# Where the second layer's weights are prepared: three units of w2_in in the last first-layer batch, the later ones one step later, five pieces of w2_out at the end of the h phase

## The chip, the cores and the metric

The kernel runs on one core of a Trainium2 chip. The metric is device time in microseconds, from the first to the last instruction of that core with what the launch adds around it. TensorE (PE) multiplies, VectorE (DVE), ScalarE (ACT) and GpSimd (POOL) do the elementwise work, and all transfers are issued from SyncE's queue (SP).

## The reference, cut to what matters

```python
x = attention(q, k, v, g_q, g_k)            # 4 batches, 12 heads, 448 tokens, 64 wide -> (1792, 768)
g = x @ w_gate;  val = x @ w_val             # 768 -> 1536
x = (g / (1 + exp(-g)) * val) @ w_out        # 1536 -> 768
h = x @ w2_in                                # 768 -> 2048
out = (h * cos(h)) @ w2_out                  # 2048 -> 768
```

The weights arrive as 64-bit floats and the results are wanted in float32, so most products are made of three fp16 matmuls on high and low halves (high x high, high x low, low x high).

## The kernel before, in words

The program has an attention part and three matmul phases. For each of the four batches the **first layer** runs 36 "pieces" of 18 matmuls: 24 of gate and val, 12 of out1 (w_out). The attention of the next batch is interleaved with it, so the last batch (the fourth) has no attention beside it; there DVE and ACT split the y results of the earlier batches instead. Then comes the **h phase** (w2_in): eight units c = 0 to 7, each two pieces of weights (k0 = 0 and 3), each used for all four batches b = 0 to 3. A step (c, b) is 36 matmuls of 448 columns into a pair of PSUM banks; four banks serve, so step n needs the banks of step n-2. I count steps from 0 to 31, step = 4c + b. At last the **out2 phase** (w2_out) multiplies the G2 tiles by 16 pieces of w2_out (two to a matmul piece).

A 64-bit weight piece goes through five stations: a load into a `raw` tile (L818), three DVE instructions that make float32 of it (L838 to L840), squares with a row sum on ACT (L858), a PE matmul that adds the rows of the unit's pieces (L865) followed by four short DVE instructions that make a power of two of the sum (L845 to L850), and a split into two fp16 halves, one instruction on ACT (L870) and one on DVE (L871). A `raw` tile is free again after the squares, because those write into it. Pieces of first use go through all this ("fresh"); a piece whose split was stored to DRAM is loaded as two halves (L892) into a `wp` tile.

`pre_step` prepares pieces ahead of their phase, one station of each of up to four pieces per call. Before, it is called 21 times (PRE: three times late in the third batch, every second piece of the fourth), and prepares all 16 pieces of w2_out as float32 in DRAM (`o32`); h pieces are not among them (NPH = 0). The h pieces are loaded at b = 0 of unit c (w_loads, L1270s), converted at b = 1, summed at b = 2 and split at b = 3, always four or five pieces ahead. The eviction of an h step (`fin_h`) is an ACT copy to integer (L1131), two DVE instructions (L1137, L1138), ACT Abs and Sin (L1139, L1140), a DVE product that reads PSUM for the last time (L1141), and the split of G2 on ACT and POOL (L1145, L1146). Its two scale rows come from a table (L1098, L1099).

The order of instructions on each engine is not the order of the code: a scheduler lays out the whole program and may put an instruction well ahead of the place where it was written. Each engine then works through its row in that order, and waits where an operand is late. SP does the same with transfers.

Of the kernel before, what the change touches and what calls it, by code (L numbers as in the profile page):

```python
# [11 lines left out]
F16 = mybir.dt.float16  # L12
# [10 lines left out]
LA = 5  # L23
CA = 4
# [8 lines left out]
CRW = 2  # L33
CSH = 10
VMQ = 2
PRE = {2: (30, 2), 3: (0, 2)}
NPH = 0
LO = 3
WSTEP = {4: [("load", 2)], 12: [("conv", 0)], 16: [("conv", 1), ("load", 3)], 19: [("scale", 1)], 20: [("split", 0), ("conv", 2), ("load", 4)],
         26: [("split", 1), ("conv", 3), ("load", 5)]}  # L40
# [99 lines left out]
def kernel(ctx: ExitStack, tc, q, k, v, g_q, g_k, w_gate, w_val, w_out, w2_in, w2_out, out):  # L140
# [23 lines left out]
    parts = {"raw": [raw_p, raw_p, raw_m], "wp": [wp_p, wp_p, wp_m]}  # L164
    turn = {"raw": 0, "wp": 0}

    def rot(nm):
        turn[nm] += 1
        return parts[nm][turn[nm] % 3]
    nm_p = ctx.enter_context(tc.tile_pool(name="nm", bufs=8))  # L170
# [616 lines left out]
    for c in range(H * D // CO):  # L787
        for b in range(0, B, 2):
            for k0 in range(0, FF2, 2):
                pieces.append(dict(kind="out2", b=b, c=c, k0=k0, n=2, first=k0 == 0, last=k0 == FF2 - 2))  # L790
    pre_load = [("out2", kt, 0) for kt in range(FF2)] + [("h", c, k0) for c in range(FF2 // 2 - NPH, FF2 // 2) for k0 in (0, 3)]
    scr = {}
    for pc in pieces:
        key = pc["key"] = (pc["kind"], pc["c"], pc["k0"])
# [10 lines left out]
    nrm_t = {}  # L805
    stores = []

    def wp_tile(dt):
        if dt == F16:
            return rot("wp").tile([P, 2, 768], F16, tag="wp", name="wp")  # L810
        return rot("wp").tile([P, 768], F32R, tag="wp", name="wp")

    sq_dst = [None]
# [60 lines left out]
    def w_load(j):  # L874
        if j >= len(pieces):
            return
        pc = pieces[j]
        if pc["kind"] == "out2" and pc["fresh"]:
            t = rot("raw").tile([P, 6 * 256], I32, tag="raw", name="raw")
            nc.sync.dma_start(t.bitcast(F32), o32[pc["k0"] // 2])  # L880
            for kk in range(2):
                w32_t[j, pc["k0"] + kk] = t[:, kk * 768:(kk + 1) * 768].bitcast(F32)
        elif pc["fresh"]:
            raw_t[j] = load64(WGT[pc["kind"]], pc["k0"], pc["c"], pc["n"], 256)
        elif pc["kind"] == "out1":
            wh, wl = wp_tile(F32R), wp_tile(F32R)
            nc.sync.dma_start(wh.bitcast(F32), scr[pc["key"]][:, 0])
            nc.sync.dma_start(wl.bitcast(F32), scr[pc["key"]][:, 1])
            wp_t[j] = (wh, wl)
        else:  # L890
            wp = wp_tile(F16)
            nc.sync.dma_start(wp, scr[pc["key"]])  # L892
            wp_t[j] = (wp[:, 0], wp[:, 1])
            wp_full[j] = wp
# [64 lines left out]
    pre_scale = []  # L959
    pre_split = []  # L960

    def pre_step():
        done = False
        if pre_split and (pre_split[0][0] == "out2" or len(pre_split) > 1):
            kind, c, k0, w32 = pre_split.pop(0)
            if kind == "h":
                for kind, c, k0, w32 in ((kind, c, k0, w32), pre_split.pop(0)):
                    stores.append((scr[kind, c, k0], split16(UNIT0[kind] + c, w32)))
            done = True
        if pre_scale and (pre_scale[0][0] == "out2" or len(pre_scale) > 1):  # L970
            kind, c, k0, w32 = pre_scale.pop(0)
            unit_scale(UNIT0[kind] + c)
            if kind == "h":
                pre_split.append((kind, c, k0, w32))
                pre_split.append(pre_scale.pop(0))
            done = True
        if pre_conv:
            kind, c, k0, rw = pre_conv.pop(0)
            w32 = conv64(rw)
            squares(UNIT0[kind] + c, w32)  # L980
            if kind == "out2":
                stores.append((o32[c // 2][:, c % 2 * 768:(c % 2 + 1) * 768], w32))
            pre_scale.append((kind, c, k0, w32))
            done = True
        if pre_load:
            kind, c, k0 = pre_load.pop(0)
            rw = load64(w2_out, c, 0, 1, 768) if kind == "out2" else load64(w2_in, k0, c, 3, 256)
            pre_conv.append((kind, c, k0, rw))
            done = True
        return done  # L990
# [212 lines left out]
    for b in range(B):  # L1203
# [14 lines left out]
        for qn in range(per):  # L1218
# [1 line left out]
            kind, c = pc["kind"], pc["c"]  # L1220
            w_store()
            w_loads(j + LA)
            if b in PRE and qn >= PRE[b][0] and (qn - PRE[b][0]) % PRE[b][1] == 0:
                pre_step()
            for i in sched.get(qn, ()):
                if b + 1 < B:
                    step(i, b + 1)
# [19 lines left out]
            wp_t.pop(j)  # L1247
            j += 1

    while pre_step():  # L1250
        w_store()
    w_store()
    g_ctx.close()
# [7 lines left out]
        y_get(B - 1, kt)  # L1261
    for kt in range(KX):
        y_split(B - 1, kt)
    w_scale(j + CA - 1)
    scaled = False
    for c in range(NH):
        j0 = j
        j += 2
        for b in range(B):
            ps = [bank(ps_m, "mm") for _ in range(2)]  # L1270
            for jj in range(j0, j):
                w_store()
                if b == 0:
                    w_loads(jj + LA)
                if b == 1:
                    w_conv(jj + CA)
                if b == 2:
                    w_scale(jj + CA)
                    if jj + CA >= N2 - 1 and not scaled:
                        out2_scales()  # L1280
                        scaled = True
                if b == 3:
                    w_split(jj + 2)
                mm_piece(jj, ps, lambda kt: Y[b, kt])
                if late:
                    late.pop(0)[1]()

            def fin(b=b, c=c, ps=ps):
                fins["h"](b, c, ps)
            if not (b == B - 1 and c == NH - 1):  # L1290
                late.append((0, fin))
            else:
                fin()
# [53 lines left out]
```

## Time and profile before

| | us |
|---|---|
| median of 3 runs (1375.33 to 1380.41) | 1379.12 |
| the profiled execution | 1378.04 |
| its span, first to last instruction | 1375.8 |
| PE busy in the span | 1198.8 (87%) |
| DVE busy | 850.9 (62%) |
| ACT busy | 658.7 (48%) |
| POOL busy | 404.5 (29%) |
| mean granted TensorE clock | 0.953 |

The profiled execution is 1.1 us below the median. The attention and first-layer part ends at 899.4 us, the h phase at about 1159, out2 at the end. A page row "idle ... <-ACT raw L858" says that the engine stood still until that instruction had ended. A "PEclk" of 1.00 is 2.4 GHz, 0.50 is 1.2 GHz.

### The profile page before, as it was taken

The numbers are of one execution on the slowest core, as the hardware profiler recorded it, in microseconds if no ns is written. First come the engines' busy times: TensorE is split into PE (matmuls) and PEld (weight loads), VectorE is DVE, ScalarE is ACT, GpSimd is POOL, SyncE is SP. The second block draws the span as 40 slices with busy tenths as digits, with TensorE's granted clock in tenths as the row PEclk, the third lists the DMA queues.
The fourth block names the chain that finished last, engine by engine and source line by source line (L and its number), as shares of the span: only waits on it lengthen the run. The fifth ranks groups of instructions, "written<-read, shape, count | busy, mean of one in ns | idle before, by whom it ended". The sixth has DMA issues, their size and how long they took to land. (4 is left out here: it accounts for less than half of the span.)

```text
span 1375.8 us, 18244 instructions
## 1 busy us (share of the span) xinstructions
PE 1198.8 (87%) x6454; PEld 676.4 (49%) x6454; DVE 850.9 (62%) x1556; ACT 658.7 (48%) x1282; POOL 404.5 (29%) x315
## 2 busy tenths in 40 slices
PE   0688677787896989999999998967999999999998
PEld 0233233334762435854458545943544555666665
DVE  6878968998947777437751676287888765200000
ACT  1567567775442645346552344265767776100000
POOL 7621345555832535214330011002233322000000
PEclk9999898788997899999999999988999999999999
DMA  7535568897999979989988988823210021633121
GB/s 233 143 81 139 183 158 245 224 247 220 287 331 286 218 172 259 302 206 203 208 190 256 322 313 274 303 74 100 73 54 24 11 62 68 217 122 98 58 87 41
DMA packets 262107, 243.93 MB, mean 177 GB/s; under 512 B 178048, under 2 KB 208256, under 8 KB 262016
## 3 DMA queue, kind: packets, MB, share of 16 engines
q1 hardware_dynamic: 262016, 242.77, 61.7%
q8 instruction: 50, 0.82, 0.2%
q14 instruction: 41, 0.34, 0.1%
HBM read 160.30 MB, written 42.51 MB: 147 GB/s over the span
## 5 line engine op out<-in xcount | busy, mean ns | idle before, releaser
L1001 PE MATMUL mm<-xy,wp 128*128 128x448 f16 x960 | 348.2, 364 | 34.2 <-DVE tmp L1141 10.0
L1002 PE MATMUL mm<-xy,wp 128*128 128x448 f16 x960 | 349.1, 364 | 0.0
L1003 PE MATMUL mm<-xy,wp 128*128 128x448 f16 x960 | 343.0, 362 | 6.0 <-DVE wp L871 5.9
L1014 PEld LDWEIGHTS <-g 128*128 128x128 f16 x1344 | 131.5, 98 | 87.3
L1001 PEld LDWEIGHTS <-wp 128*128 128x128 f16 x960 | 98.3, 102 | 121.3 <-issue 25.1
L1002 PEld LDWEIGHTS <-wp 128*128 128x128 f16 x960 | 96.3, 100 | 106.4 <-issue 30.5
L1003 PEld LDWEIGHTS <-wp 128*128 128x128 f16 x960 | 95.1, 100 | 102.5 <-issue 10.8
L1146 POOL TENSOR_TENSOR g<-tmp,g 128x448 f16<-128x448 f32 x64 | 71.5, 1136 | 230.7 <-ACT g L1145 150.8
L493 POOL TENSOR_TENSOR p<-pr,p 128x448 f16<-128x448 f32 x72 | 93.5, 1303 | 139.5 <-ACT p L484 105.3
L460 ACT ACTIVATE pr<-s,sm,esc 128x448 f32<-128x448 f32 x126 | 90.2, 718 | 67.2 <-DVE sm L454 58.5
L1001 PE MATMUL mm<-g,wp 128*128 128x448 f32 x288 | 108.8, 378 | 0.0
L1048 POOL TENSOR_TENSOR g<-tmp,g 128x448 fp32r<-128x448 f32 x48 | 63.9, 1343 | 150.5 <-ACT g L1047 150.4
L1002 PE MATMUL mm<-g,wp 128*128 128x448 f32 x288 | 106.5, 370 | 0.0
L1003 PE MATMUL mm<-g,wp 128*128 128x448 f32 x288 | 105.9, 369 | 0.0
L1014 PE MATMUL s<-wp,g 128*128 128x384 f16 x576 | 100.3, 326 | 0.0
L1014 PE MATMUL mm<-wp,g 128*128 128x384 f16 x576 | 99.2, 326 | 0.0
L450 DVE TENSOR_REDUCE sm<-s 128x1 f32<-128x448 f32 x126 | 75.4, 615 | 26.0 <-PE s L441 25.9
L484 ACT ACTIVATE p<-pr 128x448 f16<-128x448 f32 x126 | 69.8, 571 | 23.9 <-DMA PT<-p 22.8
L318 POOL TENSOR_TENSOR ri<-ss,half 128x14 f32<-128x14 f32 x24 | 63.7, 2660 | 57.2 <-DVE ss L316 48.4
L1157 ACT ACTIVATE tmp<-mm,osc 128x384 f32<-128x384 f32 x8 | 4.7, 581 | 148.6 <-PE mm L1014 147.6
L441 PE MATMUL s<-T 128*64 128x448 f16 x252 | 50.9, 394 | 26.3 <-ACT pr L460 23.3
L839 DVE SCALAR_TENSOR_TENSOR w<-raw,w 128x768 int32<-128x768 int32 x68 | 73.0, 1086 | 0.7
(170 smaller groups left out, 1988.7 us busy)
## 6 DMA issues: line engine op xcount, KB each, us to landing
wp<-scr_out SPq DMA_DIRECT2D x96, 384.0 KB, 4.1
raw<-in_moe_w_out_dram SPq DMA_DIRECT2D x28, 768.0 KB, 6.4
wp<-scr_gate SPq DMA_DIRECT2D x36, 384.0 KB, 5.3
wp<-scr_val SPq DMA_DIRECT2D x36, 384.0 KB, 5.3
raw<-in_moe_w_in_dram SPq DMA_DIRECT2D x16, 768.0 KB, 6.0
raw<-in_moe_w_gate_dram SPq DMA_DIRECT2D x12, 768.0 KB, 5.4
raw<-in_moe_w_val_dram SPq DMA_DIRECT2D x12, 768.0 KB, 4.9
scr_out<-wp SPq DMA_DIRECT2D x24, 384.0 KB, 5.4
```

What stands on the lines that cost most here:

```text
L318: nc.gpsimd.tensor_tensor(ri.rearrange("p a b -> p (a b)"), ss, half[:, :2 * NS], op=ALU.pow)
L450: nc.vector.tensor_reduce(sm[:, 0, t:t + 1], slot[n][:, :S], axis=AX.X, op=ALU.max)
L460: nc.scalar.activation(e, slot.pop(n)[:, :S], AF.Exp, bias=sm[:, 1, t:t + 1], scale=esc, accum_out=sm[:, 2, t:t + 1],)
L484: nc.scalar.activation(hi, slot[n], AF.Copy)
L493: eng.tensor_sub(p16[:, t - t0, 1], slot.pop(n), p16[:, t - t0, 0])
L839: nc.vector.scalar_tensor_tensor(wi, hi, -0x40000000, wi, op0=ALU.bitwise_and, op1=ALU.bitwise_or)
L1001: nc.tensor.matmul(ps[f][:, :S], wh[:, s], x[:, 0], start=(first and i == 0), stop=False)
L1002: nc.tensor.matmul(ps[f][:, :S], wh[:, s], x[:, 1], start=False, stop=False)
L1003: nc.tensor.matmul(ps[f][:, :S], wl[:, s], x[:, 0], start=False, stop=(last and i == n - 1))
L1014: nc.tensor.matmul(ps[:, :CO], x[:, a, p0:p0 + P], rhs, start=st, stop=sp)
L1048: nc.gpsimd.tensor_sub(x[:, 1], a, x[:, 0].bitcast(F32))
L1146: nc.gpsimd.tensor_sub(x[:, 1], r, x[:, 0])
```

## The change

The first three units of w2_in (six pieces) are put at the head of `pre_load`, are split and stored during the fourth batch, and come back as ready halves in `wp` tiles, which they take from the first of the two `wp` pools only (`base`). `pre_step` is called at every second piece of the fourth batch alone, 18 times, and loads at the first 17 of them: six h pieces and eleven of w2_out. The other five pieces of w2_out are loaded, converted and summed from step (5, 3) to step (7, 1), and `out2_scales` follows there. In the h phase, the fresh pieces of units 3 to 7 are loaded at b = 3 three units ahead, converted at b = 3 two units ahead, summed at b = 1 of the unit before and split at its b = 3. Lines of `after` are two or three higher than those of `before`.

```diff
-PRE = {2: (30, 2), 3: (0, 2)}
-NPH = 0
+NPH = 3
+PREL = 33
+HPRE = (5, 3)
...
-    def rot(nm):
+    def rot(nm, base=False):
+        if base:
+            return parts[nm][0]
...
-    pre_load = [("out2", kt, 0) for kt in range(FF2)] + [("h", c, k0) for c in range(FF2 // 2 - NPH, FF2 // 2) for k0 in (0, 3)]
+    pre_load = [("h", c, k0) for c in range(NPH) for k0 in (0, 3)] + [("out2", kt, 0) for kt in range(FF2)]
...
-            wp = wp_tile(F16)
+            wp = wp_tile(F16, pc["kind"] == "h")
             nc.sync.dma_start(wp, scr[pc["key"]])
...
-    def pre_step():
+    def pre_step(more=True):
...
-        if pre_load:
+        if pre_load and more:
...
-            if b in PRE and qn >= PRE[b][0] and (qn - PRE[b][0]) % PRE[b][1] == 0:
-                pre_step()
+            if b == B - 1 and qn % 2 == 0:
+                pre_step(qn < PREL)
...
-    w_scale(j + CA - 1)
-    scaled = False
     for c in range(NH):
...
+            if b == 1 and c:
+                w_scale(j0 + 3)
             for jj in range(j0, j):
                 w_store()
-                if b == 0:
-                    w_loads(jj + LA)
-                if b == 1:
-                    w_conv(jj + CA)
-                if b == 2:
-                    w_scale(jj + CA)
-                    if jj + CA >= N2 - 1 and not scaled:
-                        out2_scales()
-                        scaled = True
                 if b == 3:
                     w_split(jj + 2)
+                    w_conv(jj + 4)
+                    w_loads(min(jj + 6, N2 - 1))
                 mm_piece(jj, ps, lambda kt: Y[b, kt])
...
+            if (c, b) >= HPRE:
+                pre_step()
+            if (c, b) == (NH - 1, 1):
+                while pre_step():
+                    w_store()
+                out2_scales()
+                w_loads(N2 + 3)
```

The built order, at three places. First PE, between h steps 1 and 2. `s` is the bank of the sums, `nm` the row sums that ACT's squares leave; nm_8601 and nm_8650 are the two pieces of unit 2. Before:

```order
L1003 LDWEIGHTS wp_8483
L1003 MATMUL mm_8596<-xy_7819,wp_8483 128x448
L865 MATMUL s_8713<-nm_8601,full_98 128x1
L865 MATMUL s_8713<-nm_8650,full_98 128x1
L1001 LDWEIGHTS wp_8454
L1001 MATMUL mm_8670<-xy_7869,wp_8454 128x448
```

And now, where nm_8943 and nm_8992 belong to unit 3 and nm_9216 to the first piece of unit 4:

```order
L1006 LDWEIGHTS wp_8335
L1006 MATMUL mm_8562<-xy_7769,wp_8335 128x448
L868 MATMUL s_9077<-nm_8943,full_98 128x1
L868 MATMUL s_9077<-nm_8992,full_98 128x1
L868 MATMUL s_9353<-nm_9216,full_98 128x1
L1004 LDWEIGHTS wp_8333
L1004 MATMUL mm_8624<-xy_7821,wp_8333 128x448
```

The sums of unit 2 are gone from there; in their place stand both pieces of unit 3 and one of unit 4, which the code asks for seven steps later and more. The matmul of the y norm (L1065, L1068 now) stood after 45 matmuls of the h phase and now stands after 30.

Second DVE, from the last y splits (`xy`) to the eviction of step 0 (tmp_8628 and tmp_8637 before, tmp_8588 and tmp_8597 now). Before, with the two pieces w32_8646 (unit 2) and w32_8873 (unit 3):

```order
L1089 SCALAR_TENSOR_TENSOR xy_8542<-tmp_8512,ysc_105,xy_8542 128x448
L871 SCALAR_TENSOR_TENSOR wp_8741<-w32_8440,wsc_100,wp_8741 128x768
L871 SCALAR_TENSOR_TENSOR wp_8785<-w32_8477,wsc_100,wp_8785 128x768
L838 TENSOR_SCALAR w32_8646<-raw_8555 128x768
L1137 SCALAR_TENSOR_TENSOR tmp_8628<-tmp_8624,ht_8621,mm_8553 128x448
L1137 SCALAR_TENSOR_TENSOR tmp_8637<-tmp_8626,ht_8621,mm_8554 128x448
L838 TENSOR_SCALAR w32_8873<-raw_8575 128x768
L839 SCALAR_TENSOR_TENSOR w32_8646<-raw_8555,w32_8646 128x768
L1138 SCALAR_TENSOR_TENSOR tmp_8628<-tmp_8624,ht_8621,tmp_8628 128x448
L1138 SCALAR_TENSOR_TENSOR tmp_8637<-tmp_8626,ht_8621,tmp_8637 128x448
L839 SCALAR_TENSOR_TENSOR w32_8873<-raw_8575,w32_8873 128x768
L840 SCALAR_TENSOR_TENSOR w32_8646<-raw_8555,w32_8646 128x768
```

Now, with w32_9212, the first piece of unit 4:

```order
L1092 SCALAR_TENSOR_TENSOR xy_8517<-tmp_8488,ysc_105,xy_8517 128x448
L841 TENSOR_SCALAR w32_9212<-raw_8945 128x768
L1092 SCALAR_TENSOR_TENSOR xy_8520<-tmp_8490,ysc_105,xy_8520 128x448
L1140 SCALAR_TENSOR_TENSOR tmp_8588<-tmp_8584,ht_8581,mm_8523 128x448
L842 SCALAR_TENSOR_TENSOR w32_9212<-raw_8945,w32_9212 128x768
L1140 SCALAR_TENSOR_TENSOR tmp_8597<-tmp_8586,ht_8581,mm_8524 128x448
L1141 SCALAR_TENSOR_TENSOR tmp_8588<-tmp_8584,ht_8581,tmp_8588 128x448
L843 SCALAR_TENSOR_TENSOR w32_9212<-raw_8945,w32_9212 128x768
L848 TENSOR_SCALAR nm_9080<-s_9077 128x1
```

Two splits and one of the two conversions have gone from this stretch. The conversions of unit 3 stand further ahead, before the y norm.

Third DVE at step 18, the evictions of mm_9774 and mm_9775 before, of mm_9698 and mm_9699 now. Before:

```order
L1137 SCALAR_TENSOR_TENSOR tmp_9873<-tmp_9869,ht_9866,mm_9774 128x448
L1137 SCALAR_TENSOR_TENSOR tmp_9881<-tmp_9871,ht_9866,mm_9775 128x448
L1138 SCALAR_TENSOR_TENSOR tmp_9873<-tmp_9869,ht_9866,tmp_9873 128x448
L1138 SCALAR_TENSOR_TENSOR tmp_9881<-tmp_9871,ht_9866,tmp_9881 128x448
L1141 SCALAR_TENSOR_TENSOR tmp_9873<-tmp_9873,mm_9774 128x448
L1141 SCALAR_TENSOR_TENSOR tmp_9881<-tmp_9881,mm_9775 128x448
L1098 TENSOR_SCALAR ht_10217<-yhi_106,winv_99 128x2
L1099 TENSOR_SCALAR ht_10217<-yhs_107,wsc_100 128x2
```

Now:

```order
L1140 SCALAR_TENSOR_TENSOR tmp_9797<-tmp_9793,ht_9790,mm_9698 128x448
L848 TENSOR_SCALAR nm_10336<-s_10334 128x1
L1140 SCALAR_TENSOR_TENSOR tmp_9805<-tmp_9795,ht_9790,mm_9699 128x448
L1141 SCALAR_TENSOR_TENSOR tmp_9797<-tmp_9793,ht_9790,tmp_9797 128x448
L849 TENSOR_SCALAR nm_10336<-nm_10336 128x1
L1141 SCALAR_TENSOR_TENSOR tmp_9805<-tmp_9795,ht_9790,tmp_9805 128x448
L841 TENSOR_SCALAR w32_10424<-raw_10347 128x768
L852 TENSOR_SCALAR winv_99<-nm_10336 128x1
L842 SCALAR_TENSOR_TENSOR w32_10424<-raw_10347,w32_10424 128x768
L853 RECIPROCAL wsc_100<-winv_99 128x1
L1144 SCALAR_TENSOR_TENSOR tmp_9797<-tmp_9797,mm_9698 128x448
L843 SCALAR_TENSOR_TENSOR w32_10424<-raw_10347,w32_10424 128x768
```

The conversion and the power of two of two w2_out pieces stand between the instructions of the eviction. The scheduler has put these five pieces at steps 17 to 21, some five steps ahead of their place in the code. Elsewhere, from the second batch on, the order of attention instructions differs in many small places too.

## Rows read from the trace of the kernel before

**Rows 1.** Busy time by stretch: PE, PEld, DVE, ACT, POOL, PEclk, DMA share, GB/s.

```profile
760.00:899.40 139.40, 131.31 (x691) 88.12 (x690) 83.68 (x198) 53.81 (x96) 16.72 (x12) 0.99 0.83 292
914.30:926.60 12.30, 0.02 (x1) 0.00 (x0) 12.30 (x18) 9.49 (x16) 0.00 (x0) 0.63 0.00 0
926.60:931.20 4.60, 4.53 (x14) 2.09 (x15) 3.82 (x12) 3.83 (x8) 0.00 (x0) 0.50 0.74 227
942.90:953.00 10.10, 0.66 (x5) 0.50 (x4) 8.72 (x16) 7.84 (x14) 5.11 (x4) 0.77 0.26 78
953.00:958.50 5.50, 5.47 (x15) 2.23 (x15) 5.50 (x8) 3.50 (x6) 2.11 (x2) 0.50 0.00 0
```

**Rows 2.** PE in order of time, h phase: start, us, instruction [idle before, releaser].

```profile
926.67 0.59 PE L865 MATMUL s<-nm,full 128*128 128x1 f32 x2 [12.35 <-ACT raw L858]
...
942.52 0.35 PE L1002 MATMUL mm<-xy,wp 128*128 128x448 f16 x1
942.71 0.35 PE L1003 MATMUL mm<-xy,wp 128*128 128x448 f16 x1
...
945.95 0.38 PE L865 MATMUL s<-nm,full 128*128 128x1 f32 x2 [2.77 <-ACT raw L858]
953.02 0.53 PE L1001 MATMUL mm<-xy,wp 128*128 128x448 f16 x1 [6.70 <-DVE tmp L1141]
```

**Rows 3.** What PE waited for from 899 to 1160: total, times, longest.

```profile
PE s L865 <- ACT raw L858: 16.8, 3, 12.4
PE mm L1001 <- DVE tmp L1141: 10.0, 6, 6.7
```

**Rows 4.** Groups from 899 to 1160: count, busy us, mean ns, idle before.

```profile
L1138 DVE SCALAR_TENSOR_TENSOR tmp<-tmp,ht 128x448 f32<-128x448 int32 x62 | 43.2, 725 | 0.1
L1137 DVE SCALAR_TENSOR_TENSOR tmp<-tmp,ht,mm 128x448 f32<-128x448 int32 x64 | 41.2, 673 | 18.1 <-ACT tmp L1131 17.0 <-POOL g L1146 0.9
L1131 ACT ACTIVATE tmp<-mm,ht 128x448 int32<-128x448 f32 x64 | 38.3, 626 | 14.1 <-PE mm L1003 8.6 <-POOL g L1146 5.2
L1141 DVE SCALAR_TENSOR_TENSOR tmp<-tmp,mm 128x448 f32<-128x448 f32 x62 | 38.3, 619 | 29.1 <-ACT tmp L1140 28.3
L1099 DVE TENSOR_SCALAR ht<-yhs,wsc 128x2 f32<-128x2 f32 x29 | 18.9, 656 | 0.0
L871 DVE SCALAR_TENSOR_TENSOR wp<-w,wsc,wp 128x768 f16<-128x768 f32 x16 | 16.1, 1022 | 0.2 <-ACT wp L870 0.2
L839 DVE SCALAR_TENSOR_TENSOR w<-raw,w 128x768 int32<-128x768 int32 x13 | 12.7, 987 | 0.0
L840 DVE SCALAR_TENSOR_TENSOR w<-raw,w 128x768 int32<-128x768 int32 x13 | 12.2, 947 | 0.0
L1098 DVE TENSOR_SCALAR ht<-yhi,winv 128x2 f32<-128x2 f32 x29 | 11.1, 384 | 0.0
L858 ACT ACTIVATE raw<-w 128x768 f32<-128x768 f32 x13 | 10.9, 838 | 5.1 <-DVE w L840 3.0 <-issue 2.0
L838 DVE TENSOR_SCALAR w<-raw 128x768 int32<-128x768 int32 x13 | 8.8, 682 | 0.6 <-DMA raw<-in_moe_w_in_dram 0.6
L1088 ACT ACTIVATE xy<-tmp,ysc 128x448 f16<-128x448 f32 x6 | 5.8, 1054 | 4.2 <-DVE ysc L850 4.2
```

**Rows 5.** ACT in order of time before PE's release at 926.67.

```profile
921.89 1.17 ACT L1139 ACTIVATE tmp<-tmp 128x448 f32<-128x448 f32 x2 [2.76 <-DVE tmp L1138]
923.09 1.28 ACT L1140 ACT_TABLE_LOAD   x1
924.38 1.41 ACT L1140 ACTIVATE tmp<-tmp,hpi,ht 128x448 f32<-128x448 f32 x2
925.70 0.83 ACT L858 ACTIVATE raw<-w 128x768 f32<-128x768 f32 x1
```

**Rows 6.** PE in order of time: the two longest stops of the fourth batch.

```profile
826.84 0.38 PE L1065 MATMUL s<-nm,full 128*128 128x1 f32 x2 [2.44 <-DVE nm L1063]
...
839.54 0.53 PE L1001 MATMUL mm<-xy,wp 128*128 128x448 f16 x1 [3.53 <-DVE tmp L1037]
```

More of the change, by code (lines that the diff above doesn't have):

```diff
@@ L806, with wp_tile @@
     stores = []
-    def wp_tile(dt):
+    def wp_tile(dt, base=False):
         if dt == F16:
-            return rot("wp").tile([P, 2, 768], F16, tag="wp", name="wp")
+            return rot("wp", base).tile([P, 2, 768], F16, tag="wp", name="wp")
         return rot("wp").tile([P, 768], F32R, tag="wp", name="wp")
@@ L1248 @@
             j += 1
-    while pre_step():
+    while pre_step(False):
         w_store()
```

## The prediction

> **What bounds the kernel now.** I read the busy time by stretch first, to find where PE is not full, then PE's own rows in order of time, to see what it stood still for, then its waits by releaser, and last the groups of the h phase for prices. PE is the bound nearly everywhere: in the fourth batch it is busy 131.31 of 139.40 us [rows 1]. The exception is the start of the h phase. There PE stops three times: 12.35 us until ACT's squares of unit 2 are there, 2.77 us for those of units 3 and 4, and 6.70 us until DVE has given back a bank [rows 2], 21.8 us together. The reader should see that these are most of what PE loses to these two causes in the whole phase, 16.8 and 10.0 us [rows 3], and that DVE is busy for all of 12.30 us of the first stop [rows 1]: it has y splits, weight splits, two conversions and two evictions in its queue at once. The stops cost a second time: after each, PE works at 1.2 GHz, a granted clock of 0.50, for 4.60 and 5.50 us [rows 1], where it gets half done. That is (4.60 + 5.50) / 2 = 5.05 us more. What the change can take away at most is therefore 21.8 + 5.05 = 26.9 us.
>
> **The change, part by part.** I write times from the start of the h phase, 899.4. A matmul takes one place each 0.19 us (942.52 to 942.71) [rows 2], a step of 36 takes 6.84.
>
> *The stop at step 2.* Before, it began at +14.9 and ended at 926.67, +27.3. The halves of units 0 to 2 are now ready, so nothing that steps 2 to 11 multiply by has to be made here. But the scheduler has put three sums in the place of the two: unit 3 twice and the first piece of unit 4, and PE takes its row in order. The pieces of unit 3 are converted ahead of the y norm and their squares stand on ACT ahead of the y splits, so they are no wait. The piece of unit 4 is. Its chain: the y norm comes after 30 matmuls, +5.7; before it came after 45, +8.6, and I take the same 1.6 us from there to ACT's first y split as an estimate, between nothing and the 4.2 us that ACT stood waiting for it [rows 4]. So ACT starts at +7.3. Six y splits take 5.8 us [rows 4], to +13.1; four copies (L1131) at 0.626 overlap a little, to +15.3. DVE ends the last y split 1 us after ACT, at +14.1, and then does two L1137, one L839, one L1138 and one L840 of the new piece: 2 x 0.673 + 0.987 + 0.725 + 0.947 = 4.0, some 0.4 less by overlap: L1138 ends at +16.7 and the conversion at +17.7. ACT has Abs of step 0 at +17.3, the load of the Sin table 1.28 [rows 5], one Sin of 0.7 (1.41 for two [rows 5]), at +19.3, and then the squares, 0.838 [rows 4] and 0.2 of read-out as an estimate: +20.3. PE is there after 72 matmuls and the small sums, at +14.2. The stop is 6.1 us. Bounds: 2.5 if ACT's squares come as soon as the conversion is done and the bank of step 0 is the last wait, 12.4 if the chain is as long as now. 6.1 is a walk through the built order, so I take it. After it I put 2 us for work at half clock, from the 2.3 that the first stop cost.
>
> On the table load the trace shows 1.28 us and the next ACT instruction 1.29 us after its start [rows 5]. The Trainium skill, "ScalarE: Activation LUTs", section "What ACT_TABLE_LOAD costs", gives about 1.28 us for the load and about 1.38 us of drain for every switch; with that drain the stop would be 7.5 and the time 1.4 us later, but the row shows no drain, so the sum goes without it.
>
> *The stops at step 4.* The sums that stood there (2.77) are not in the new row at step 4. The bank wait of 6.70 came from DVE, which had two conversions and two splits beside the evictions; in the new row the next conversion stands at steps 3 to 5. I put 1 us for steps 4 and 5, between 0 and 6.7.
>
> *Steady h phase.* Conversions: 13 in the phase before [rows 4], now 15 in all (units 3 to 7 and the five of w2_out), of which two stand before the y splits; splits 16 before, 10 now. DVE's sum is the same within 6 us of 260. The new timing (load, conversion, sum and split each later against the use, by whole steps) costs nothing so long as a piece has two steps, 13.7 us, between stations; its own work on DVE and ACT is 2.62 and about 1 us.
>
> *Five w2_out pieces at steps 17 to 21.* There was no weight work there beyond unit 7's. A step's evictions are 2 x (0.673 + 0.725 + 0.619) = 4.03 us on DVE, its table rows 0.384 + 0.656 = 1.04, one conversion 0.682 + 0.987 + 0.947 = 2.62 [rows 4]: 7.69 against PE's 6.84. The excess of 0.85 five times is 4.3 us; I take 4.5 with the short power-of-two rows. Below: 0, if overlap of DVE's instructions (about 0.09 each) closes it. Above: 18, if each conversion with its squares (2.62 + 1.03) delays PE in full. The value is nearer the lower end because DVE was not full in these steps. If DVE were, the cover of PE's 6.84 us would be gone and each piece would cost the 3.6.
>
> The row for L1099 has a mean of 656 ns and that for L1098 384, the same size of work [rows 4]; they run when POOL works. The Trainium skill, "SBUF — State Buffer", section "SBUF: two separate sides", says that VectorE and GpSimd share one port pair as an exclusive lock, held for a whole instruction. That speaks against putting conversions between evictions, whose G2 half POOL makes: if every first conversion step waited once for as long as it runs (0.68), five would cost 3.4 us more, which my upper bound holds.
>
> *The fourth batch.* Removed: three conversions from the end of the third and from the fourth batch in sum (20 before with the first h pieces, 17 now), 3 x 2.62 = 7.9 us of DVE; added: four splits, 4 x 1.02 = 4.1 [rows 4], six stores and six loads of 384 KB while the DMA share is 0.83 [rows 1], against five raw tiles fewer of w2_out. PE stops there twice for over 2 us, 2.44 and 3.53, both behind DVE [rows 6]. The longer one has four y splits and a conversion ahead of the eviction in both orders, so it stays. I give the shorter one back nearly whole: -2.2; bounds +4 (a stop like the 3.53 more) and -6 (both gone).
>
> *SP.* The six loads of halves stand behind the last out1 loads and wait for `wp` tiles that out1's last pieces free; a piece is 18 matmuls, 3.6 us, and the two that step 0 needs are issued two or three pieces before the end. Five microseconds of landing fit. Price if not: the first step late by some 3 us.
>
> Sum: 1378.04 - 21.8 - 5.05 + 6.1 + 2 + 1 + 4.5 - 2.2 = 1362.6 on the profiled execution; the median stands 1.1 higher: 1363.7. I say 1363.
>
> **The rivals.** *Nothing is won, the wait moves.* The piece of unit 4 ends as late as unit 2's did (12.35), PE is at half clock as long, and the bank wait of 6.70 comes back behind it: 6.3 + 0.3 + 5.7 more, 1376, the same within half a percent. For it: the three sums are as early in PE's row as the two were. Against: the two splits and one conversion that left DVE's queue, and the norm that is 15 matmuls earlier.
>
> *Slower.* The five pieces turn PE's in-order sums into five stops. Two `raw` tiles give each piece two steps, 13.7 us, for landing, its turn on DVE (up to one step, 6.84), 2.62 of conversion, its turn on ACT and the squares. If that does not fit, each stop costs what one for L858 cost on average, 16.8 / 3 = 5.6 [rows 3], and 2.5 at half clock: 5 x 8.1 = 40 in place of 4.5, so 1399. It decides from about 4 us a piece. Against it: before, the same chain in the steady phase made one short stop, 16.8 - 12.35 - 2.77 = 1.7 us [rows 2, 3].
>
> *Better.* The late pieces hide and both stops of the fourth batch go: -4.5 - 3.8, and no bank wait: 1354.
>
> **How the numbers follow.** Forecast 0.64, no gain 0.15, slower 0.07, better 0.14. The changed order of the attention, whose price no row shows, adds 3 us either way. The forecast's own bounds (stop at step 2 from 2.5 to 12.4, late pieces from 0) give 1356 to 1374; with better and no gain in part, the range is 1352 to 1375. About half a percent, 6.9 us, is what a measurement can tell: under 1372.2 is faster. Nearly all of forecast (0.62) and better fall there, 0.76; no gain and the rest, 0.16; slower 0.08.
>
> **What would show it.** Right: the first stop of the h phase is at step 2, about 6 us, released by the squares on ACT; no stop over 3 us at steps 4 and 5; the clock falls once there, not twice; small bank waits on L1144 around steps 17 to 21; the h phase some 13 us shorter. Wrong: stops on L868 at steps 18 to 21, a stop at step 0 on a `wp` load, or a fourth batch longer than 139 us by more than 3.

## The result, and the profile after

The changed kernel takes 1361.19 us (median of 4 runs, 1359.69 to 1366.4) against 1377.96 for the kernel before on the same chip: a ratio of 0.9888, 95% interval 0.9859 to 0.9916. A second set of 4 runs gave 1359.9 and 0.9871 (0.983 to 0.9912). So it is 1.1 to 1.3% faster. The prediction was 1363, and "faster" was its likeliest case.

To see where the time went, cut both profiled executions at the first matmul of each stage, and read the busy time of every stretch. (The first matmuls of the second batch stand among the last ones of the first; the cut is 3.5 us after them in every kernel.) Columns: start:end, length, then busy us (and instructions) of PE, PEld, DVE, ACT and POOL, the granted clock, the DMA share, GB/s. The rows are the second, third and fourth batch and the h phase. Before:

```profile
395.20:590.40 195.20, 169.10 (x934) 99.74 (x933) 122.25 (x253) 85.00 (x192) 69.23 (x49) 0.93 0.95 256
590.40:760.90 170.50, 165.39 (x954) 95.78 (x954) 88.99 (x187) 82.10 (x188) 49.60 (x41) 0.99 0.88 212
760.90:899.80 138.90, 130.81 (x688) 87.48 (x687) 84.08 (x198) 53.61 (x97) 16.72 (x12) 0.99 0.82 290
899.80:1158.70 258.90, 232.10 (x1215) 121.04 (x1215) 201.07 (x358) 179.91 (x307) 68.59 (x62) 0.95 0.18 56
```

After:

```profile
396.10:584.30 188.20, 167.25 (x933) 99.01 (x932) 122.18 (x252) 85.06 (x191) 67.37 (x49) 0.95 0.95 254
584.30:753.60 169.30, 163.75 (x950) 94.83 (x949) 87.95 (x184) 81.59 (x187) 49.75 (x41) 1.00 0.91 218
753.60:892.50 138.90, 132.33 (x687) 88.05 (x687) 89.52 (x187) 55.70 (x97) 16.42 (x12) 0.98 0.85 298
892.50:1140.30 247.80, 230.17 (x1218) 120.47 (x1217) 201.70 (x372) 176.50 (x307) 71.00 (x62) 0.99 0.24 79
```

The reader should see three things. The h phase, which the change is about, is 11.1 us shorter. The fourth batch, where the new work went, is as long as before, with 5.4 us more of DVE. And the second batch, whose code the change does not touch, is 7.0 us shorter.

What PE waited for in the h phase of after (total, times, longest), the answer to [rows 3]:

```profile
PE mm L1004 <- DVE tmp L1144: 9.0, 11, 2.0
PE s L868 <- ACT raw L861: 8.6, 2, 6.7
```

The waits for squares fell from 16.8 to 8.6 us; those for a bank are 9.0 in place of 10.0, but now eleven small ones and no long one. In order of time, PE's longest stops of after, which answer to [rows 2] (start, us, instruction, idle before and its releaser):

```profile
913.56 0.59 PE L868 MATMUL s<-nm,full 128*128 128x1 f32 x2 [6.67 <-ACT raw L861]
...
967.57 0.38 PE L868 MATMUL s<-nm,full 128*128 128x1 f32 x2 [1.89 <-ACT raw L861]
...
998.30 0.35 PE L1004 MATMUL mm<-xy,wp 128*128 128x448 f16 x1 [2.00 <-DVE tmp L1144]
...
1029.24 0.35 PE L1004 MATMUL mm<-xy,wp 128*128 128x448 f16 x1 [1.99 <-DVE tmp L1144]
1037.61 0.35 PE L1004 MATMUL mm<-xy,wp 128*128 128x448 f16 x1 [1.15 <-DVE tmp L1144]
...
1060.34 0.35 PE L1004 MATMUL mm<-xy,wp 128*128 128x448 f16 x1 [1.45 <-DVE tmp L1144]
```

They stand at steps 2, 9, 13, 17, 18 and 21. Before, there were 12.35 at step 2, 2.77 and 6.70 at step 4, and 1.69 and 2.00 at steps 13 and 17. The clock falls once: 0.50 from 911.6 to 918.4.

The chain behind the stop at step 2 is read on ACT, from the y splits to the squares that release PE:

```profile
899.39 5.88 ACT L1091 ACTIVATE xy<-tmp,ysc 128x448 f16<-128x448 f32 x6 [2.71 <-DVE ysc L853]
905.17 1.66 ACT L1134 ACTIVATE tmp<-mm,ht 128x448 int32<-128x448 f32 x3
...
910.03 0.58 ACT L1142 ACTIVATE tmp<-tmp 128x448 f32<-128x448 f32 x1 [1.96 <-DVE tmp L1141]
910.63 1.28 ACT L1143 ACT_TABLE_LOAD   x1
911.92 0.76 ACT L1143 ACTIVATE tmp<-tmp,hpi,ht 128x448 f32<-128x448 f32 x1
912.59 0.83 ACT L861 ACTIVATE raw<-w 128x768 f32<-128x768 f32 x1
913.32 0.19 ACT L861 ACTIVATION_READ_ACCUMULATOR raw<-w 128x1 f32 x1
```

Step 2 needs a second thing as well, the bank of step 0. DVE's first instruction of that eviction and the product that reads the bank for the last time are these:

```profile
907.27 0.68 DVE L1140 SCALAR_TENSOR_TENSOR tmp<-tmp,ht,mm 128x448 f32<-128x448 int32 x1
...
912.72 0.62 DVE L1144 SCALAR_TENSOR_TENSOR tmp<-tmp,mm 128x448 f32<-128x448 f32 x1 [0.53 <-ACT tmp L1143]
```

The product ends at 913.34, the squares release PE at 913.56. So the two ends of this stop lie 0.2 us apart, and the row names only the later one.

### The profile page after: what moved, and what is told of

It reads as the page before. It is cut to its first block, busy times and chain, and to the rows that moved or that the text cites. A ratio compares the mean times of both kernels' runs of the same rounds, so it can differ in the third digit from the quotient of the medians.

```text
span 1357.6 us, 18256 instructions
## 1 busy us (share of the span) xinstructions
PE 1195.9 (88%) x6454; PEld 674.9 (50%) x6454; DVE 856.4 (63%) x1556; ACT 657.2 (48%) x1282; POOL 405.9 (30%) x315
## 4 chain that ended last, share of the span: by engine, by line
PE 46%; DVE 16%; DMA 7%; ACT 4%; issue 3%; SPq 1%; POOL 0%; ACTq 0%; DVEq 0%; POOLq 0%
PE mm L1004 9%; PE mm L1006 9%; PE mm L1005 9%; PE mm L1017 7%; PE s L1017 7%; PE t L1017 2%; DVE w L842 2%; DVE w L843 2%; DMA T<-h 2%; PE t L555 2%; DMA PT<-p 2%; PE s L444 1%; DVE tmp L1140 1%; DVE w L841 1%; DVE tmp L1141 1%
## 5 line engine op out<-in xcount | busy, mean ns | idle before, releaser
L487 ACT ACTIVATE p<-pr 128x448 f16<-128x448 f32 x126 | 69.5, 570 | 21.5 <-DMA PT<-p 20.6
```

The source lines that it names most:

```text
L487: nc.scalar.activation(hi, slot[n], AF.Copy)
```

## The experiments

The table gives the length of each stage in the profiled execution, read from PE's row as above, and the time (before: median of the runs beside after; after, after again, one unit, no late piece, one sum in both layers, and the last two: median of 4 runs; the others: one run). "Late" are the pieces of w2_out that are prepared inside the h phase; "PE still" is the length of the second batch less PE's busy time in it.

| kernel | units ahead | late | second | PE still in it | third | fourth | h phase | time |
|---|---|---|---|---|---|---|---|---|
| before | 0 | 0 | 195.2 | 26.1 | 170.5 | 138.9 | 258.9 | 1377.96 |
| before again | 0 | 0 | 197.0 | 28.0 | 172.9 | 137.4 | 258.9 | 1382.7 |
| new places alone | 0 | 0 | 195.1 | 22.0 | 170.1 | 136.1 | 258.6 | 1376.84 |
| one unit, one late piece | 1 | 1 | 192.8 | 21.9 | 168.3 | 131.3 | 247.1 | 1358.39 |
| one unit | 1 | 0 | 191.6 | 23.2 | 170.4 | 132.0 | 246.6 | 1357.11 |
| two units | 2 | 3 | 188.8 | 20.1 | 170.3 | 138.5 | 248.0 | 1358.18 |
| after | 3 | 5 | 188.2 | 21.0 | 169.3 | 138.9 | 247.8 | 1361.19 |
| after again | 3 | 5 | 189.2 | 20.6 | 168.4 | 137.1 | 248.3 | 1359.9 |
| no late piece | 3 | 0 | 188.7 | 21.0 | 173.3 | 130.8 | 244.2 | 1353.46 |
| no late piece, old places | 3 | 0 | 192.2 | 21.0 | 170.4 | 134.4 | 244.7 | 1357.09 |
| one sum, both layers | 3 | 5 | 194.4 | 23.5 | 169.5 | 133.0 | 243.8 | 1359.67 |
| one sum | 3 | 5 | 193.5 | 22.4 | 170.8 | 133.3 | 243.6 | 1359.76 |
| one sum, two units | 2 | 0 | 188.8 | 20.7 | 171.6 | 135.2 | 245.7 | 1357.78 |
| one sum, no late piece | 3 | 0 | 190.7 | 21.9 | 170.3 | 136.0 | 239.3 | 1349.93 |

One thing about the method stands in the column of the h phase: it repeats within 0.6 us (258.9 and 258.9; 247.8 and 248.3), so differences of 1 us there mean something. The attention batches do not repeat that well.

**Both kernels again.** Theory: the second batch is shorter because its instructions are laid out in another order; rival: it varies from one execution to the next.

> The changed kernel once more, unchanged. Its first profile has the second batch 188.2 us long and the third 169.3 where the kernel before has 195.2 and 170.5, and the h phase 247.8 where the kernel before has 258.9. Theory A: the shorter second batch comes from the order in which the scheduler now lays out the attention; then it is again 187 to 190 us here, the h phase again 247 to 249, and the time near 1361. Theory B: the second batch varies from execution to execution; then it comes out anywhere from 187 to 196 and the time with it.

> The kernel before once more, unchanged. Theory A (the order of the attention decides): the second batch is again 194 to 197 us and the h phase 258 to 260. Theory B (variation between executions): the second batch is somewhere from 187 to 196.

Measured: after 189.2, before 197.0; h phase 248.3 and 258.9. The two kernels keep their difference. What PE waited for in the second batch, before and then after:

```profile
PE s L441 <- ACT pr L460: 10.0, 7, 3.0
PE t L552 <- DMA PT<-p: 9.1, 4, 3.0
PE s L343 <- DVE vrow L340: 3.1, 1, 3.1
```

```profile
PE s L444 <- ACT pr L463: 7.8, 7, 2.3
PE t L555 <- DMA PT<-p: 6.6, 3, 2.8
...
PE s L346 <- DVE vrow L343: 1.3, 1, 1.3
```

They are the same waits in the attention, 6.5 us less in sum. In all PE stands still for 21.0 us in place of 26.1, and again for 20.6 in place of 28.0. The rest of the first pair's 7.0 is PE's own busy time (169.10 to 167.25), at a granted clock of 0.95 in place of 0.93. Two pairs cannot part the two theories; the last section does it with all kernels.

**The new places alone.** The title of the change has two halves: units split ahead, and later ones "one step later". This kernel keeps the second half and drops the first.

```diff
-NPH = 3
+NPH = 0
...
-            if b == 1 and c:
+            if b == 1:
                 w_scale(j0 + 3)
```

> The changed kernel without any unit of w2_in split ahead (and so without late pieces of w2_out): of the change only the later places of load, conversion, sum and split in the h phase are left. In the built order this kernel's rows are those of the kernel before with its three preparing steps of the third batch moved into the fourth, but for tile numbers and one load on SP. Theory A: the later places are written in the code and undone by the scheduler, so they do nothing: the stops of 12 and 7 us are back and the h phase is 257 to 261 us. Theory B: the late places matter by the load on SP; then the h phase is 247 to 253.

Measured: an h phase of 258.6. Its waits of PE in the h phase are those of [rows 3] to the last digit:

```profile
PE s L868 <- ACT raw L861: 16.8, 3, 12.4
PE mm L1004 <- DVE tmp L1144: 10.0, 6, 6.7
```

Theory A holds: the later places alone do nothing. In the h phase the trace has the same instructions in the same order as before on PE, DVE, ACT and POOL.

**Units ahead with the old places.** The other way round, and without late pieces:

```diff
...
+                if b == 0:
+                    w_loads(jj + LA)
+                if b == 1:
+                    w_conv(jj + CA)
+                if b == 2:
+                    w_scale(jj + CA)
...
                 if b == 3:
                     w_split(jj + 2)
-                    w_conv(jj + 4)
-                    w_loads(min(jj + 6, N2 - 1))
...
```

> The kernel with three units split ahead and no late piece, but with the kernel before's places for load, conversion, sum and split in the h phase. Its rows are those of the kernel with the new places and no late piece, but for tile numbers and one load on SP. Theory A: the same h phase as there, 243.5 to 245, and the same stop of 6.5 us at step 2. Theory B: loads that are written earlier delay something; h phase 247 or more.

Measured: 244.7 us, against 244.2 with the new places, and the same waits, 8.1 us for squares and 6.3 for banks against 8.2 and 6.3. The scheduler builds the same rows on PE, DVE, ACT and POOL from both codes; only one load on SP stands elsewhere. So the whole gain of the h phase comes from the units split ahead.

**How many units.** Three kernels vary the number.

> The changed kernel with one unit of w2_in split ahead in place of three, and one late piece of w2_out in place of five. The sums of unit 2 stand at steps 1 and 2 of PE's row again. Theory A: the units split ahead are what took the stops away; then stops of 10 us and more in sum come back at steps 1 to 5, the clock falls twice, and the h phase is 255 to 262 us although four late pieces (about 0.75 us each by the kernel without any) are gone from it. Theory B: the later timing of the other pieces did it; then the stops stay near 7 us and the h phase near 245.

> The changed kernel with two units of w2_in split ahead, and three late pieces. The sums of unit 3 stand at steps 2 and 2.5 of PE's row. Theory A (units split ahead count): the stop at step 2 is 9 to 13 us, its chain holding the conversions of unit 3, and the h phase is 250 to 255. Theory B (the timing counts): a stop of 6 to 7 us and an h phase of 245 to 247.

> One unit of w2_in split ahead and all sixteen pieces of w2_out before the h phase, so that the count of units alone is compared: none gave an h phase of 258.6, three gave 244.2 and 244.7, each without late pieces. Theory A: the first unit takes away nearly all, since it takes two conversions and two splits from DVE where the evictions of the first steps wait; h phase 246 to 248, the stop near step 2 below 8 us, no stop over 3 us at steps 4 and 5, and the time 1353 to 1358. Theory B: each unit gives a like share; then about 254, and the stops at steps 4 and 5 are back by half.

In the first two theory A was that stops of 9 us and more come back; its sizes were wrong both times (stops at step 2 of 6.55 and 5.04 us, h phases of 247.1 and 248.0). Theory B, the timing, falls with the kernel that has the new places alone. The third compares the count alone, without late pieces: none 258.6, one 246.6, three 244.2. The first unit brings 12.0 of the 14.4 us. ACT's first y split and DVE's row at the start of the h phase show why. Before:

```profile
909.56 5.84 ACT L1088 ACTIVATE xy<-tmp,ysc 128x448 f16<-128x448 f32 x6 [4.18 <-DVE ysc L850]
910.67 5.75 DVE L1089 SCALAR_TENSOR_TENSOR xy<-tmp,ysc,xy 128x448 f16<-128x448 f32 x6
916.34 1.94 DVE L871 SCALAR_TENSOR_TENSOR wp<-w,wsc,wp 128x768 f16<-128x768 f32 x2
918.20 0.55 DVE L838 TENSOR_SCALAR w<-raw 128x768 int32<-128x768 int32 x1
918.66 1.26 DVE L1137 SCALAR_TENSOR_TENSOR tmp<-tmp,ht,mm 128x448 f32<-128x448 int32 x2
```

With one unit ahead:

```profile
897.56 3.96 ACT L1091 ACTIVATE xy<-tmp,ysc 128x448 f16<-128x448 f32 x4 [4.80 <-DVE ysc L853]
...
904.25 0.67 DVE L1140 SCALAR_TENSOR_TENSOR tmp<-tmp,ht,mm 128x448 f32<-128x448 int32 x1
...
906.93 1.94 DVE L874 SCALAR_TENSOR_TENSOR wp<-w,wsc,wp 128x768 f16<-128x768 f32 x2
```

The eviction of step 0 starts 13.1 us after the first matmul of the phase (891.18), not 18.8 (899.83). Of these 5.7 us some 2.4 are the two weight splits (1.94) and the first instruction of a conversion, which no longer stand ahead of it. The other 3.3 come from the y splits: ACT begins them 6.4 us after the first matmul and not 9.7, because PE's row has the y norm after 28 matmuls in place of 45. No run has one of the two without the other. What is left of the stop at step 2 is then a wait for a bank, 5.53 us, and the two stops at step 4 are gone.

**One sum for a unit.** To test what holds PE at step 2 of after, the row sums of a unit's two pieces are added on DVE, and PE makes one sum in place of two, which therefore cannot stand ahead of the second piece.

```diff
+        if UNIT0["h"] <= u < UNIT0["out2"]:
+            nc.vector.tensor_tensor(q[0][:, 1:2], q[0][:, 0:1], q[1][:, 0:1], op=ALU.add)
+            q = [q[0][:, 1:2]]
...
-            nc.tensor.matmul(ps[:, :1], full, n[:, 0:1], start=(i == 0), stop=(i == len(q) - 1))
+            nc.tensor.matmul(ps[:, :1], full, n, start=(i == 0), stop=(i == len(q) - 1))
```

The first of the two kernels below did this in both layers, the second in w2_in alone, as in the diff.

> The changed kernel, but the two row sums of a unit are added on DVE first and PE makes one sum for each unit in place of two. The sum of the first piece of unit 4 can then no longer stand in PE's row ahead of the second piece's squares, so it should leave step 2. Theory A: the stop of 6.9 us at step 2 is the wait for that one sum; it shrinks to between 2.5 and 4 us, where the bank that step 0 gives back decides, and the kernel is 3 to 6 us faster than the changed one, about 1356. Theory B: DVE and ACT are that late in any case, and the evictions of step 0 hold PE just as long; then a stop of 5 to 7 us stands at steps 2 to 4 with another releaser, and the time stays at 1361.

> The changed kernel with one PE sum for each unit of w2_in, its two row sums added on DVE first; the first layer is left as it is. In the built order the sum of unit 4 now stands at step 5.5 and not, by half, at step 2. Theory A: the stop at step 2 was the wait for that half sum; what is left there is 3 to 4 us, for the bank of step 0, and the h phase is 243 to 245 against 247.8. The edit that did the same in the first layer too had an h phase of 243.8, but a second batch of 194.3. Theory B for that: adding on DVE in the first layer changed the attention; then the second batch is 187 to 190 here and the time near 1356. Rival: any edit may lay the attention out anew, and the second batch is anywhere from 188 to 197.

In both, the h phase is 4 us shorter (243.8 and 243.6), and the stop at step 2 is 3.4 us: the sizes that theory A gave. But the edit changed more than the sum. In DVE's row the eviction of step 0 now stands behind four y splits and no longer behind six, as these rows of the second kernel show:

```profile
908.40 0.67 DVE L1145 SCALAR_TENSOR_TENSOR tmp<-tmp,ht,mm 128x448 f32<-128x448 int32 x1
...
913.89 0.61 DVE L1149 SCALAR_TENSOR_TENSOR tmp<-tmp,mm 128x448 f32<-128x448 f32 x1
914.56 0.53 PE L1009 MATMUL mm<-xy,wp 128*128 128x448 f16 x1 [3.40 <-DVE tmp L1149]
```

Counted from the first matmul of the phase (892.64 in after, 897.13 here), the eviction starts at 11.3 us in place of 14.6, the bank is back at 17.4 in place of 20.7, and step 2 begins at 17.4 in place of 21.4. So the missing half sum gave 0.7 of the 4 us, and the earlier eviction 3.3. In each of the seven kernels whose step 2 waits for no squares PE goes on within 0.1 us of that product's end. That the stop was the wait for the half sum, as theory A has it, is therefore not shown: without it the bank would have held PE nearly as long. No run moves the sum alone.

The second kernel's waits of PE in the h phase are one row, with no wait for squares left:

```profile
PE mm L1009 <- DVE tmp L1149: 15.8, 11, 3.4
```

Yet neither kernel is faster than after: their second batch took 194.4 and 193.5 us. The guess that adding on DVE in the first layer had done this fell with the second kernel, which leaves the first layer as it is. The rival, that the edit laid the attention out anew, falls for the second kernel as well: its second batch has the same instructions in the same order as that of after, on PE, DVE, ACT, POOL and SP. Of the 5.3 us, 3.7 are PE's busy time, 170.97 us at a granted clock of 0.92, where after has 167.25 at 0.95:

```profile
399.50:592.90 193.40, 170.97 (x933) 100.43 (x931) 122.57 (x252) 84.76 (x192) 67.48 (x49) 0.92 0.95 249
```

So the second kernel's longer batch comes of the execution and not of the edit (last section). The first kernel does have another row there, and what that costs stays open.

**No late piece.** All 16 pieces of w2_out are prepared ahead; five preparing steps move into the end of the third batch.

```diff
-            if b == B - 1 and qn % 2 == 0:
-                pre_step(qn < PREL)
+            if (b == B - 1 or b == B - 2 and qn >= 26) and qn % 2 == 0:
+                pre_step(b < B - 1 or qn < PREL)
```

> The changed kernel with all sixteen pieces of w2_out prepared before the h phase: five more preparing steps stand in the end of the third batch and none in the h phase. Theory A: the five late pieces cost what the prediction put on them, 4.5 us in steps 17 to 21; then the h phase is 243 to 244 us in place of 247.8, and the third and fourth batch grow by 0 to 4. Theory B: the late pieces are hidden but for 1 to 2 us; then the h phase is 246 to 248. In both the stop at step 2 stays at 6 to 7 us.

Measured: h phase 244.2, so the five pieces cost 3.6 to 4.1 us (3.1 to 3.6 by the 244.7 of the kernel above, which has the same rows). Of the eleven bank waits of after, 9.0 us, eight are left, 6.3 us. Gone are the stops at steps 18, 19 and 21: 1.15, 0.17 and 1.45 us. The one at step 17 stays, 1.99 us; it is there before, too, at 2.00. The third batch grew by 4 to 5 us and the fourth shrank by 6 to 8, while the kernel with the same rows but one, above, had 170.4 and 134.4: the two batches together are 304.1 and 304.8, against 308.2 and 305.5 in after. In the same set of runs it beats after by 6.4 us (1353.46, range 1351.84 to 1354.88, against 1359.9); the single run of the kernel with the old places was 1357.09.

**Both together, and with two units.**

> Both edits together: one sum for each unit of w2_in, and all sixteen pieces of w2_out prepared before the h phase. Theory A: the two gains in the h phase, 4.0 and 3.6 us, have different places (step 2, steps 17 to 21) and add: h phase 240 to 241, and 1349 to 1351 if the second batch stays at 188 to 190. Theory B: with the stop at step 2 gone PE only waits later, for banks; h phase 243 to 244, time near 1353.

> Two units of w2_in split ahead, one PE sum for each unit, all pieces of w2_out before the h phase. One and three units ahead gave 247.1 and 247.8 with one and five late pieces; at 0.73 us a late piece that is 246.4 and 244.1, so a unit is worth about 1 us. Theory A: h phase 240 to 241.5 against 239.3 with three units, the fourth batch no longer than 136, and the time 1347 to 1352, as the second batch is laid out. Theory B: the sum of unit 3 at step 4 brings a stop of 5 us or more; h phase 244 or more.

The two gains add: 239.3 us, and 1349.93 (1347.59 to 1352.0), a ratio to before of 0.979 (0.9759 to 0.9821). This is the fastest of all, and better than after by about 10 us. With two units the h phase is 245.7, outside the 240 to 241.5 that was expected, and stops of 6.42 and 3.27 us stand at steps 2 and 6. There all six y splits stand ahead of the first eviction, and DVE then idles for ACT:

```profile
899.08 5.81 DVE L1097 SCALAR_TENSOR_TENSOR xy<-tmp,ysc,xy 128x448 f16<-128x448 f32 x6
904.80 1.26 DVE L1145 SCALAR_TENSOR_TENSOR tmp<-tmp,ht,mm 128x448 f32<-128x448 int32 x2
...
911.19 0.62 DVE L1149 SCALAR_TENSOR_TENSOR tmp<-tmp,mm 128x448 f32<-128x448 f32 x1 [1.18 <-ACT tmp L1148]
```

The bank of step 0 comes back 20.4 us after the first matmul of the phase, where the kernel with three units has 17.4. So a unit is not worth a fixed amount: what counts is which row the scheduler makes of it, and at step 2 where that row has the first eviction. Why it puts the evictions there was not traced.

## Why the prediction was right, and where it was not

**The stops at the start of the h phase.** Predicted -21.8 + 6.1 + 1. All stops of the first eight steps, from PE's row: 21.8 us before, 6.9 after, -14.9 against -14.7. The stop at step 2 is 6.67 by its releaser's row, not 6.1. The walk had L1138 of step 0 (L1141 now) end at +16.7, and it ended 0.7 later, at +17.4, because two things stand ahead of DVE's last y split that the walk left out, L841 and a wait for its load:

```profile
905.90 0.56 DVE L841 TENSOR_SCALAR w<-raw 128x768 int32<-128x768 int32 x1 [0.57 <-DMA raw<-in_moe_w_in_dram]
...
909.32 0.68 DVE L1141 SCALAR_TENSOR_TENSOR tmp<-tmp,ht 128x448 f32<-128x448 int32 x1
```

The releaser is the one that was named, by 0.2 us. The lower bound of 2.5 is wrong: it has the bank of step 0 back at +16.7, while the same walk ends the conversion at +17.7 and Sin at +19.3, and the product that frees the bank comes after Sin. The product ended at +20.7. Without the half sum this row would have stopped PE for some 6.5 us all the same (an estimate: 913.34 less the start of the stop, 906.89). That 3.4 us were left in the one-sum kernels, near that bound, is luck: there the eviction stands earlier. Sin follows the table load after 1.29 us again; by the drain in the Trainium skill's "ScalarE: Activation LUTs" ("What ACT_TABLE_LOAD costs") it would have come about 1.38 us later.

**Half clock: mis-sized by 1 us.** Predicted -5.05 + 2. The clock stays at 0.50 for 4.8 us after the stop, by which 2.4 us of work are lost. PE's busy time in the phase, where the loss is counted, fell by 1.9 us (232.10 to 230.17), not by 3.05.

**Late pieces.** Predicted 4.5, measured 3.1 to 4.1, of which 2.8 are bank waits at steps 18 to 21. The rival of 40 us did not come: no wait for squares stands there. The port lock that the Trainium skill's "SBUF — State Buffer" ("SBUF: two separate sides") describes was weighed at 3.4 us more, 7.9 in all; the measured cost is about half of that. The trace of before agrees with a lock in the table rows: of 18 L1099 that ran while POOL worked, 15 took 1.05 to 1.10 us, and all 11 that ran without it 0.22. But the first instruction of the five late conversions (L841 from 1029.11 to 1054.70) took 0.55 to 0.56 us each time, and POOL worked during none of them.

**The steady h phase: the mis-sized term.** The prediction gave it nothing, because DVE's sum is the same, and it is (201.07 and 201.70; the 260 of the prediction is the length of the phase). But stops at steps 8 to 17 rose from 5.0 to 7.9 us, in after and equally in the kernel without late pieces, +2.9. The stop at 967.57 is 1.89 of them: a sum waits for squares whose conversion stands on DVE between the instructions of an eviction.

```profile
960.57 1.28 DVE L841 TENSOR_SCALAR w<-raw 128x768 int32<-128x768 int32 x1
...
965.60 0.94 DVE L843 SCALAR_TENSOR_TENSOR w<-raw,w 128x768 int32<-128x768 int32 x1
966.58 0.84 ACT L861 ACTIVATE raw<-w 128x768 f32<-128x768 f32 x1 [0.42 <-DVE w L843]
```

From its first instruction to its end this conversion took 6.0 us, where its own work is 2.62. An equal sum of work says nothing of where it stands. So the h phase gave 11.1 us, not 13.3: stops -14.9, +2.9 and +2.8, PE's busy time -1.9.

**The fourth batch: mis-sized too.** Predicted -2.2, measured 0.0 (138.9 twice; 137.4 and 137.1 again). The 7.9 us taken from DVE were three conversions counted over two batches; the fourth itself converts 15 pieces before and after, and has four splits more. The two stops of [rows 6] became one:

```profile
830.49 0.53 PE L1004 MATMUL mm<-xy,wp 128*128 128x448 f16 x1 [5.55 <-DVE tmp L1040]
```

Its waits are 6.6 us in all against 8.1, but after them the clock is at 0.50 for 6.8 us in place of 3.4, half of which is lost: that takes the 1.5 back. Neither is fixed by the amount of work: the one-sum kernels have the same conversions and splits there in another order, and take 133.0 and 133.3 us.

**The order of the attention: the term that made the number come out.** It was priced at 3 us either way. The second batch gave 7.0 and the third 1.2 in the first pair, 7.8 and 4.5 in the second. By all executions the order of the second batch is worth about 6 us (last section). No row had given this term a size or a sign, so that it came out as a gain, and this large, is luck. These 8 us made up for 2.2 missing in the h phase and 2.2 in the fourth batch. Without them the same kernel would have taken about 1369, still in the range, so the number came out closer than its parts. (The first batch, 0.9 us longer, is the rest.)

**The reason for the gain.** "Nothing that steps 2 to 11 multiply by has to be made here" is true, but it is not what pays. Twelve of the 14.4 us come with the first unit. With it the first eviction starts 5.7 us earlier, by the splits and the conversion that are gone from its way and by the earlier y norm. The prediction named both, but as what speaks against a rival and as a start of its walk, not as what sets the stop. And the new places in the h phase, which it costed at nothing because two steps are enough time, cost nothing because the built rows do not change.

## What to carry to other kernels

Where a scheduler lays out the rows, compare the built rows of each half of a change by itself before giving it a price: a half that leaves them as they are can be crossed out. Price the work that stands ahead of the first late instruction rather than the sum of an engine's work, and expect that an edit in one stage has others laid out anew. Ask of a stop what would end it if the releaser that the profile names came earlier: at step 2 the bank would have held PE to within 0.2 us as long as the squares did. After a gain, look at what was moved to pay for it: here five late pieces and the late place of the first eviction cost some 8 us that two small edits won back.

## What the runs showed of the hardware

The same rows do not take the same time twice in the attention. The second batch of the two kernels with three units and no late piece, new places and then old ones:

```profile
395.60:584.30 188.70, 167.68 (x934) 98.84 (x933) 121.94 (x250) 86.01 (x194) 67.19 (x49) 0.95 0.94 252
```

```profile
396.10:588.20 192.10, 171.14 (x933) 100.34 (x931) 121.98 (x251) 85.98 (x194) 67.41 (x48) 0.92 0.94 249
```

The 3.4 us are PE's busy time (171.14 against 167.68) at a granted clock of 0.92 in place of 0.95; every other engine is the same, and PE stands still for 21.0 us in both. So PE's busy time in a batch varies by some 3 us from one execution to the next. The time still varies as well. The kernel with the new places alone has, in its second batch, the instructions of before in the order of before (but for two short ones on DVE), and there PE stands still for 22.0 us, where before has 26.1 and 28.0, and is busy for longer:

```profile
398.10:593.20 195.10, 173.12 (x933) 100.87 (x931) 122.92 (x256) 84.64 (x190) 68.63 (x48) 0.90 0.96 255
```

All kernels together tell what the order is worth. The order of before stands in three profiled executions: 195.1 to 197.0 us, mean 195.8. The order of after, but for a few short instructions, stands in eight (after, after again, two units, no late piece with new and with old places, one sum in w2_in alone, and the last two of the table): 188.2 to 193.5 us, mean 190.0. No execution of one order reaches the other, so the order is worth about 6 us, and a single pair of executions shows anything from 1.6 to 8.8.

The clock after a short stop differs as well. After the stops of 1.9 and 0.2 us at step 9, which the second execution of after and the first share, the granted clock was 0.50 for 3.41 us in the one (first row) and full in the other:

```profile
964.84:968.25 3.41, 3.41 (x11) 1.40 (x10) 3.41 (x8) 2.42 (x6) 2.22 (x2) 0.50 0.62 213
```

```profile
967.57:971.00 3.43, 3.19 (x17) 1.77 (x18) 3.43 (x8) 3.00 (x6) 1.31 (x1) 1.00 0.66 192
```
